# Attention's first two units by pairs of heads, with a new order of the whole program

## The chip, the cores and the metric

The kernel runs on one core of a Trainium2 chip. The metric is the device time of one launch in microseconds (us). A core has five engines that run side by side, each through its own queue in program order: TensorE (PE; its weight loads are PEld) multiplies matrices, VectorE (DVE) and ScalarE (ACT) work on elements, GpSimd (POOL) does the same more slowly, and SyncE (SP) issues the loads and stores (DMAs). PSUM is the memory that TensorE writes its results to; SBUF holds everything else.

## The reference

Local attention with block summaries, then two feed-forward layers, all in fp32.

```python
# q, k, v: (2, 8, 768, 64); block = 32, window = 16
k_sum = k.reshape(B, H, nb, block, D).max(axis=3)
v_sum = v.reshape(B, H, nb, block, D).mean(axis=3)
scores_l = where(abs(i - j) < window, scale * q @ k.T, -1e9)
scores_s = scale * q @ k_sum.T + log(block)
a = softmax(concat(scores_l, scores_s))
x = a @ concat(v, v_sum)                 # reshaped to 1536 tokens x 512
h = x @ w_in                             # 512 x 2048
P = a0 + a1*h + a2*h*h + a3*h**3
Q = 1 + abs(b0)*abs(h) + abs(b1)*h*h
x = (P / (Q + 1e-6)) @ w_out             # 2048 x 512
h = x @ w_in2
out = (h * cos(h)) @ w_out2
```

## The kernel before

**Attention** is cut into units u of 128 queries, all eight heads at once as four pairs (a pair has 2 x 64 = 128 partitions). For the first batch, `k_pair` loads the keys of a pair in two halves of 384 (L454), TensorE turns a half around by six matmuls against the identity, a key group (L463), ScalarE or VectorE copies the result from PSUM into the tile `big` (`cp`, L322 on ScalarE, L324 on GpSimd, L327 on VectorE), and VectorE reduces it to block maxima (L471). `q_tile` brings the queries: for units 0 and 1, one load for heads 0 to 3 and one for heads 4 to 7 hold both units (L559); TensorE turns all four pairs around into one PSUM tile `qtp` of 128x512 (L432), and one copy takes that to `qT`. Later units load `qk` and use L577.

`attn_a` gathers for a unit the 24 block maxima of each head (one copy for all pairs) and the keys in the windows of its two halves of 64 queries (128x768 elements, one copy or two) into `room`, of which there are two sets. Then TensorE makes the scores of all pairs, 16 matmuls into two PSUM tiles `sp` (L626). VectorE masks them pair by pair and takes the minimum (L641; 8 a unit), ScalarE takes the exp (L645), both add and invert the sums (L650, L652, L655), and GpSimd or VectorE multiplies (L658). `attn_b` turns the weights around (`ptp`, L672), `attn_c` loads the values `vw` (L707), multiplies (`avp`, L719) and splits the result into a high and a low part, `xH` and `xL` (L730). `v_mean0` loads v of the first batch (L507), adds neighbours (L514) and makes the block means.

**The layers** multiply in three products of reduced precision (xH with w, xL with w, xH with the low part of w). Weights come as 64 bit floats (`raw`, loaded at L415) and are converted by VectorE in three instructions per 512 columns (L745, L749, L753), cast, and their low part taken on GpSimd or VectorE (L762). `h` is L849 in the first layer and L947 in the second, the second product `acc` is L1091. `co` holds the coefficients (loaded at L380, L381).

**The order.** The functions above do not issue instructions; they write operations with what they read and write into a plan. `ORDER`, a table of numbers (L56), then says for every place in the program which operation comes next and which engine takes it; `add_a` sets the order in which operations are written, on which the table counts. Dependences between operations are kept for named parts of a resource (`Res`), in the plan; the waits in the program are set by what the instructions touch in the tiles. The early PSUM tiles (`ktp`, `qtp`, `sp` and so on, up to unit 1) take the buffers acc0 to acc3 and ps in turn.

## Time and profile before

| | us |
|---|---|
| median of 3 runs (lowest, highest) | 602.42 (601.41 to 603.23) |
| the profiled execution | 601.51 |
| its span | 599.40 |
| outside the span | 2.11 |
| PE busy | 586.1 (98%) |
| DVE busy | 547.9 (91%) |
| ACT busy | 434.2 (72%) |
| POOL busy | 331.8 (55%) |

A row of the stretches gives the busy time of each engine in it, its instructions, the TensorE clock that was granted as a share of full speed, the busy share of the DMA engines and what they moved. A row of the timeline is an instruction or a run of like ones, with its start and its time; in brackets is the idle time of the engine just before it and what ended that. A row of the chain of waits is a piece of the work that ended last. The profile and the times show one core only.

### The profile page before, as it was taken

Reading aid. Unit: us, or ns where it says so; the run is one execution under the profiler, and the core shown is the slowest. Engines: PE = TensorE matmul, PEld = TensorE weight load, DVE = VectorE, ACT = ScalarE, POOL = GpSimd, SP = SyncE. Lnnn points to the kernel's source line nnn. Section 1 sums busy time; section 2 is a strip of 40 time slices with the busy share of each in tenths; the row PEclk is TensorE's granted clock in tenths of the full one; section 3 lists DMA queues with packets and bytes.
Section 4 is the critical chain, followed back from the end, with each engine's and each line's share of the span. In section 5 each row is a group of like instructions: output and inputs, shape, how many; then the busy total and the mean of one; then the engine's idle time right before and its main releaser. Section 6 shows DMA issues by size and latency. Waiting matters only on the chain.

```text
span 599.4 us, 10768 instructions
## 1 busy us (share of the span) xinstructions
PE 586.1 (98%) x3843; PEld 499.7 (83%) x3843; DVE 547.9 (91%) x1082; ACT 434.2 (72%) x940; POOL 331.8 (55%) x317
## 2 busy tenths in 40 slices
PE   8779999999999999999999999999999999999997
PEld 8468878788888888888888888889899989999886
DVE  5899999879999999989999999999889899899784
ACT  3889999677686866887688887675677557754463
POOL 5576876467673666578687733454356617424020
PEclk9899999999999999999999999999999999999999
DMA  8997865200321223321311222021130322200013
GB/s 255 243 240 194 218 185 144 61 1 1 106 71 39 71 68 105 106 71 36 95 46 35 62 80 70 2 71 57 49 107 31 101 78 73 72 1 0 19 71 123
DMA packets 68861, 51.84 MB, mean 86 GB/s; under 512 B 37304, under 2 KB 63160, under 8 KB 68808
## 3 DMA queue, kind: packets, MB, share of 16 engines
q1 hardware_dynamic: 68664, 51.03, 28.8%
q8 instruction: 30, 0.49, 0.3%
q14 instruction: 23, 0.19, 0.1%
q10 hardware_dynamic: 144, 0.13, 0.1%
HBM read 47.71 MB, written 3.15 MB: 85 GB/s over the span
## 4 chain that ended last, share of the span: by engine, by line
PE 89%; DVE 6%; SPq 2%; DMA 1%; ACT 1%; issue 0%; DVEq 0%
PE acc L1091 44%; PE h L849 26%; PE h L947 15%; PE avp L719 1%; PE ptp L672 1%; DMA raw<-in_moe_w_in_dram 1%; PE sp L626 1%; DVE sc L641 1%; DVE f L749 1%; SPq L507 1%; SPq L454 1%; DVE f L753 1%; PE vmp L542 0%; PE qtp L577 0%; DVE f L745 0%
## 5 line engine op out<-in xcount | busy, mean ns | idle before, releaser
L1091 PE MATMUL acc<-gh,w 128*128 128x512 f32 (+1 forms) x416 | 122.8, 378 | 0.0
L1091 PE MATMUL acc<-w,gh 128*128 128x512 f32 x382 | 119.1, 393 | 0.0
L849 PE MATMUL h<-xH,w 128*128 128x512 f32 (+1 forms) x352 | 110.0, 373 | 0.3 <-DVE big L495 0.3
L762 POOL TENSOR_TENSOR gl<-te,gh 128x512 fp32r<-128x512 f32 (+1 forms) x57 | 75.8, 1331 | 47.7 <-ACT gh L322 27.1
L1091 PEld LDWEIGHTS acc<-gh,w 128*128 128x128 f32 x416 | 75.6, 188 | 15.3 <-issue 1.3
L762 POOL TENSOR_TENSOR w<-f,w 128x512 fp32r<-128x512 f32 x47 | 66.3, 1412 | 31.5 <-ACT w L322 25.5
L1008 POOL TENSOR_TENSOR tu<-tu,tf 128x512 f32<-128x512 f32 (+1 forms) x48 | 61.7, 1286 | 32.6 <-ACT tf L1000 31.8
L1091 PE MATMUL acc<-gl,w 128*128 128x512 f32 (+1 forms) x208 | 77.5, 373 | 0.0
L1091 PEld LDWEIGHTS acc<-w,gh 128*128 128x128 f32 x382 | 66.9, 189 | 9.6
L849 PEld LDWEIGHTS h<-xH,w 128*128 128x128 f32 x352 | 64.5, 188 | 12.4 <-DVE big L495 0.5
L1091 PE MATMUL acc<-w,gl 128*128 128x512 f32 x191 | 74.3, 389 | 0.0
L849 PE MATMUL h<-xL,w 128*128 128x512 f32 (+1 forms) x176 | 65.1, 370 | 0.0
L849 PE MATMUL h<-big,w 128*128 128x512 f32 x240 | 58.1, 389 | 0.0
L849 PEld LDWEIGHTS h<-big,w 128*128 128x128 f32 x240 | 45.1, 188 | 9.3
L749 DVE SCALAR_TENSOR_TENSOR f<-raw,f 128x512 int32<-128x512 int32 x64 | 51.1, 800 | 0.4
L753 DVE SCALAR_TENSOR_TENSOR f<-raw,f 128x512 int32<-128x512 int32 x64 | 47.5, 746 | 0.4
L324 POOL TENSOR_SCALAR gh<-te 128x512 fp32r<-128x512 f32 (+1 forms) x26 | 18.9, 728 | 51.0 <-DVE te L1054 20.2
L1091 PEld LDWEIGHTS acc<-gl,w 128*128 128x128 f32 x208 | 39.1, 188 | 6.9
L1049 ACT ACTIVATE h<-h 128x512 f32<-128x512 f32 x48 | 27.9, 582 | 20.7 <-DVE h L1046 20.3
L1091 PEld LDWEIGHTS acc<-w,gl 128*128 128x128 f32 x191 | 35.9, 188 | 7.9
L998 ACT ACTIVATE tu<-h,co 128x512 f32<-128x512 f32 (+1 forms) x52 | 33.6, 651 | 10.9 <-PE h L849 10.8
L1018 ACT ACTIVATE h<-tf 128x512 f32<-128x512 f32 (+1 forms) x52 | 29.7, 571 | 16.2 <-DVE te L1012 15.6
(219 smaller groups left out, 1458.9 us busy)
## 6 DMA issues: line engine op xcount, KB each, us to landing
raw<-in_moe_w_in_dram SPq DMA_DIRECT2D x32, 512.0 KB, 3.7
raw<-in_moe_w_out_dram SPq DMA_DIRECT2D x32, 512.0 KB, 5.1
vw<-in_v_dram SPq DMA_DIRECT2D x24, 192.0 KB, 4.2
qk<-in_q_dram SPq DMA_DIRECT2D x10, 256.0 KB, 5.4
out_dram<-part SPq DMA_DIRECT2D x8, 256.0 KB, 2.0
part<-in_k_dram SPq DMA_DIRECT2D x8, 192.0 KB, 4.0
big<-in_v_dram SPq DMA_DIRECT2D x3, 512.0 KB, 6.6
qk<-in_k_dram SPq DMA_DIRECT2D x6, 256.0 KB, 5.2
```

The lines of the kernel that those rows point to most:

```text
L324: nc.gpsimd.tensor_scalar(out=o, in0=i, scalar1=1.0, scalar2=1.0, op0=ALU.mult, op1=ALU.mult)
L454: lambda e, i=i, rt=rt: nc.sync.dma_start(out=rt(), in_=k[0, 2 * pr:2 * pr + 2, 384 * i:384 * i + 384].rearrange("h (s j) d -> s h (j d)", ...
L749: lambda e: nc.vector.scalar_tensor_tensor(out=ft.t.bitcast(I32), in0=lohi()[1], scalar=-0x40000000, in1=ft.t.bitcast(I32), op0=ALU.bitwis ...
L753: lambda e: nc.vector.scalar_tensor_tensor(out=ft.t.bitcast(I32), in0=lohi()[0], scalar=29, in1=ft.t.bitcast(I32), op0=ALU.logical_shift_r ...
L762: lambda e: E[e].tensor_tensor(out=lo(), in0=x(), in1=hi().bitcast(F32), op=ALU.subtract),
L849: nc.tensor.matmul(out=h.t[:, 0:n], lhsT=lt, rhs=rt[:, kk, cs], start=(k0 == 0 and i == 0), stop=(k0 == 2 and i == 5))
L947: nc.tensor.matmul(out=bank.t[:, c], lhsT=lt, rhs=rt, start=start and i == 0, stop=stop and i == 5, skip_group_check=True)
L998: lambda e: nc.scalar.activation(out=U(), in_=H(), func=ACTF.Square, scale=b1s))
L1008: lambda e: E[e].tensor_tensor(out=U(), in0=U(), in1=Z(), op=ALU.add))
L1018: lambda e: nc.scalar.activation(out=H(), in_=Z(), func=ACTF.Exp, scale=-1.0))
L1049: lambda e: nc.scalar.activation(out=H(), in_=H(), func=ACTF.Abs))
L1091: nc.tensor.matmul(out=dst, lhsT=lt, rhs=rt, start=(un.start and not have and i == 0), stop=(un.stop and i == 2), skip_group_check=have)
```

## The change

`q_tile` for units 0 and 1 makes its transposes and its copy in two halves (pairs 0 and 1, pairs 2 and 3), each half a resource of its own; `attn_a` for these units gathers the block maxima and the windows pair by pair and makes the scores of a pair as soon as its keys and its half of q are there; a mask depends on its pair's scores alone. `add_a` writes `q_tile` of unit 0 behind the first pair of keys. The table `ORDER` is a new one for the whole program, in order and in choice of engine.

```diff
 ORDER = (
-    "c-rk)+mED2bw5?7>bqaMze``fzD@V^^i0pCcRV|L@p^5~nzfg)*S3V$2HUcTu`#SkSm(k;$bcU}0*r`+M8rdau!L}ADT"
...
+    "c-rk*OOIXIRbKmX_IW?=dEMu^kE&bmD&O*>+HH4L+pe}v((P6|3QoE^Qq%4{h(gjhiIfDApcX+4NJk)~NGM8BW)2915s"
...
@@ q_tile
+        dst = qTs[u % NQ]
         if u < 2:
...
+            for i in range(2):
+                def tr(e, i=i):
+                    for x in range(2):
+                        transpose_pairs(tp.t[:, 2 * i + x, :], q_first[i][1]()[:, 2 * x:2 * x + 2], 64 * u, 64)
+
+                P.op([("T", 0.44)], [q_first[i][0]], [tp[i], dst[i]], tr)
+                P.op([("A", act(256, True)), ("V", dve(256))], [tp[i]], [dst[i]],
+                     lambda e, i=i: cp(e, dst.t[:, 2 * i:2 * i + 2], tp.t[:, 2 * i:2 * i + 2]))
+            P.now += 0.88
+            return
...
@@ attn_a
+        every = range(NP)
+
+        def gather(prs):
+            sl = slice(prs[0], prs[-1] + 1)
+            np_ = len(prs)
+            kks = {kr["k", i, y] for w in ws for i in range(w // 128, (w + WK - 1) // 128 + 1) for y in prs}
...
+            if t < NKW:
+                sums = [kr[x] for x in kr.subs if x[0] == "s" and x[1] in prs]
+                P.op([("P", Shared(0.6 if np_ == NP else 0.22)), ("A", act(48 * np_))], sums, [kw["s", y] for y in prs],
+                     lambda e: cp(e, kw.t[:, sl, :, WK:KW],
+                                  ks()[:, sl].unsqueeze(2).to_broadcast([128, np_, 2, NB])))
+            n = 192 * np_
+            P.op([("P", Shared(0.85 if np_ == NP else 0.18 + n * 0.00087)), ("A", act(n)), ("V", dvef(n))],
+                 sorted(kks, key=id), [kw["w", y] for y in prs], windows)
+            P.op([("T", SPT * np_ / NP)], [qt[i] for i in sorted({y // 2 for y in prs})] + [kw[x, y] for x in "sw" for y in prs],
+                 [sp[y] for sp in sps for y in prs], mm)
+
+        if u < 2:
+            for y in every:
+                gather([y])
+        else:
+            gather(list(every))
...
-                P.op([("V", 0.19)], [sp, m], [sc[pr], mn[hh, pr]],
+                P.op([("V", 0.19)], [sp[pr], m], [sc[pr], mn[hh, pr]],
...
@@ add_a
         if u == 0:
-            for i in range(NP):
+            fill.append((k_pair, 0, 30.0))
+            fill.append((q_tile, 0, 30.0))
+            for i in range(1, NP):
                 fill.append((k_pair, i, 30.0))
...
-        fill.append((q_tile, u, 30.0 if u < 2 else 8.0))
+        if u:
+            fill.append((q_tile, u, 30.0 if u < 2 else 8.0))
```

Three places show how the new table moves instructions; the lines of the changed code are by one to 16 higher. The first is TensorE at the start of the program, before: key groups (`ktp`) up to the last two, then the transposes of q; in brackets is what an instruction waits for.

```order
L463 MATMUL ktp<-ident,part 64x128 [waits DMAHW6_49,DVE_49]
L463 MATMUL ktp<-ident,part 64x128 x5
L463 MATMUL ktp<-ident,part 64x128 [waits DMAHW7_49,DVE_49]
L463 MATMUL ktp<-ident,part 64x128 x5
L432 MATMUL qtp<-ident,part 64x64 [waits DMAHW1_49,DVE_49]
L432 MATMUL qtp<-ident,part 64x64 x7
L432 MATMUL qtp<-ident,part 64x64 [waits DMAHW0_49]
L432 MATMUL qtp<-ident,part 64x64 x7
```

And the changed program, TensorE from the first key group, and, behind "...", from the first scores to the last key group:

```order
L464 MATMUL ktp<-ident,part 64x128 [waits DMAHW2_49]
L464 MATMUL ktp<-ident,part 64x128 x5
L433 MATMUL qtp<-ident,part 64x64 [waits DMAHW3_49,DVE_49]
L433 MATMUL qtp<-ident,part 64x64 x7
...
L627 MATMUL sp_273<-room,qT_203 64x120 [waits Activation_49]
...
L433 MATMUL qtp<-ident,part 64x64 [waits DVE_49]
L433 MATMUL qtp<-ident,part 64x64 x7
L433 MATMUL qtp<-ident,part 64x64 [waits Activation_49]
L433 MATMUL qtp<-ident,part 64x64 x7
L464 MATMUL ktp<-ident,part 64x128 [waits DMAHW1_49,DVE_49,PE_49]
L464 MATMUL ktp<-ident,part 64x128 x5
```

All four halves of q and the scores of unit 0's first pair now stand ahead of the last key group; the second half of unit 0 waits for VectorE, that of unit 1 for ScalarE. Second, ScalarE at the start, before: copies of key groups, the block maxima into `room`, one copy of q, and then the exps (L645).

```order
L330 ACT_TABLE_LOAD
L322 COPY big<-ktp 128x384 x5
L322 COPY room<-big 128x8x24
L322 COPY qT_307<-qtp 128x512
L645 ACTIVATE sc,su<-sc,mn 128x120 x11
L322 COPY qT_282<-qtp 128x512
```

And changed, from the third key copy to the copy of q for unit 2:

```order
L323 COPY big<-ktp 128x384
L323 COPY room<-big 128x2x24
L323 COPY big<-ktp 128x384
L323 COPY qT_289<-qtp 128x256 x2
L323 COPY room<-big 128x2x24 x3
L323 COPY room<-big 128x96 x2
L323 COPY big<-ktp 128x384
L323 COPY room<-big 128x2x24 x2
L661 ACTIVATE sc,su<-sc,mn 128x120 x11
L323 COPY qT_203<-qtp 128x512
```

Five small copies stand between the second half of unit 1's q and the last copy of keys, two more behind it, and the exps come after. Third, SyncE's loads, before: keys, q, v, the q of unit 2 (`qk`), the coefficients, the first w_in (`raw`).

```order
L454 DMA part<-in_k_dram 128x2x192 x8
L559 DMA part<-in_q_dram 128x4x128 x2
L507 DMA big<-in_v_dram 128x8x128 x3
L415 DMA qk<-in_q_dram 128x8x64
L380 DMA co<-in_moe_a_dram 128x4
L415 DMA raw<-in_moe_w_in_dram 128x4x128
L707 DMA vw_356<-in_v_dram 96x8x64
```

And changed:

```order
L455 DMA part<-in_k_dram 128x2x192
L560 DMA part<-in_q_dram 128x4x128
L455 DMA part<-in_k_dram 128x2x192
L560 DMA part<-in_q_dram 128x4x128
L455 DMA part<-in_k_dram 128x2x192 x6
L508 DMA big<-in_v_dram 128x8x128 x3
L416 DMA raw<-in_moe_w_in_dram 128x4x128
L381 DMA co<-in_moe_a_dram 128x4
L416 DMA qk<-in_q_dram 128x8x64
L723 DMA vw_388<-in_v_dram 96x8x64
```

The loads of q stand behind the first and the second piece of keys, and w_in and the q of unit 2 have changed places. Of the window copies, those of units 0 and 1 are now 96 or 2x96 columns wide and spread over the three engines; the 128x768 copies of units 2, 3 and 4 are on GpSimd, VectorE and ScalarE, where they were on GpSimd, GpSimd and ScalarE.

## Rows read from the trace of the kernel before

**Rows 1.** Page, and stretches: window, us, busy PE PEld DVE ACT POOL, PEclk, DMA

```profile
PE 586.1 (98%) x3843; PEld 499.7 (83%) x3843; DVE 547.9 (91%) x1082; ACT 434.2 (72%) x940; POOL 331.8 (55%) x317
60.00:590.00 530.00, 529.88 (x3123) 453.12 (x3121) 494.77 (x888) 387.11 (x776) 293.53 (x252) 1.00 0.23 69
```

**Rows 2.** Stretches from 20 to 60 us

```profile
20.00:25.00 5.00, 3.42 (x67) 3.05 (x68) 4.43 (x18) 4.17 (x15) 1.58 (x2) 0.80 0.77 210
...
30.00:60.00 30.00, 25.62 (x331) 22.09 (x332) 29.77 (x110) 28.06 (x102) 22.19 (x27) 1.00 0.83 217
```

**Rows 3.** Chain of waits, 5 to 32 us: start, us, what

```profile
10.85 1.45 SPq L415
...
13.87 6.61 DMA raw<-in_moe_w_in_dram
```

**Rows 4.** Timeline of PE: start, us, line and operation, [idle before, releaser]

```profile
5.14 6.00 PE L463 MATMUL ktp<-ident,part 128*64 128x128 f32 x96
11.07 1.91 PE L432 MATMUL qtp<-ident,part 64*64 64x64 f32 x64
13.11 1.87 PE L626 MATMUL sp<-room,qT 64*64 64x120 f32 x64
...
17.78 0.66 PE L577 MATMUL qtp<-ident,qk 128*128 128x128 f32 x4
...
23.22 2.17 PE L719 MATMUL avp<-pt,vw 120*64 120x64 f32 x32 [0.88 <-DMA vw<-in_v_dram]
...
27.61 1.15 PE L719 MATMUL avp<-pt,vw 120*64 120x64 f32 x30 [0.17 <-ACT pt L322]
...
31.11 0.38 PE L849 MATMUL h<-xH,w 128*128 128x256 f32 x1
```

**Rows 5.** Timeline of DVE, the same columns

```profile
6.44 0.56 DVE L327 COPY big<-ktp 128x384 f32<-128x384 f32 x1 [6.44 <-PE ktp L463]
6.92 0.55 DVE L471 TENSOR_REDUCE big<-ktp 128x12 f32<-128x384 f32 x1
...
13.94 0.69 DVE L514 TENSOR_TENSOR big<-big 128x512 f32<-128x512 f32 x1 [0.38 <-DMA big<-in_v_dram]
14.55 0.27 DVE L641 CUSTOM_DVE_ANT_0 sc<-sp,room 128x120 f32<-128x120 f32 x1
...
17.27 0.31 DVE L652 TENSOR_SCALAR su<-su 128x4 f32<-128x4 f32 x1 [0.21 <-ACT sc L645]
...
20.50 0.43 DVE L745 TENSOR_SCALAR f<-raw 128x512 int32<-128x512 int32 x1 [0.99 <-DMA raw<-in_moe_w_in_dram]
...
23.91 0.40 DVE L327 CAST w<-f 128x512 fp32r<-128x512 f32 x1
```

**Rows 6.** Timeline of ACT, the same columns

```profile
10.53 0.48 ACT L322 COPY big<-ktp 128x384 f32<-128x384 f32 x1 [0.18 <-PE ktp L463]
11.18 0.48 ACT L322 COPY big<-ktp 128x384 f32<-128x384 f32 x1 [0.18 <-PE ktp L463]
12.28 0.35 ACT L322 COPY room<-big 128x192 f32<-128x192 f32 x1 [0.62 <-DVE big L471]
...
14.86 0.40 ACT L645 ACTIVATE sc<-sc,mn 128x120 f32<-128x120 f32 x1 [1.25 <-DVE mn L641]
...
19.04 0.56 ACT L322 COPY qT<-qtp 128x512 f32<-128x512 f32 x1
...
21.29 0.39 ACT L645 ACTIVATE sc<-sc,mn 128x120 f32<-128x120 f32 x1 [0.55 <-DVE mn L641]
...
23.27 0.21 ACT L650 ACTIVATE su<-su 128x4 f32<-128x4 f32 x1
23.37 0.82 ACT L322 COPY room<-big 128x768 f32<-128x768 f32 x1
```

**Rows 7.** Page, DMA issues: instruction, count, KB each, median us to landing

```profile
raw<-in_moe_w_in_dram SPq DMA_DIRECT2D x32, 512.0 KB, 3.7
...
qk<-in_q_dram SPq DMA_DIRECT2D x10, 256.0 KB, 5.4
```

More of the change, by code (lines that the diff above doesn't have):

```diff
@@ L618, in attn_a @@
-        n = 768
-        P.op([("P", Shared(0.85)), ("A", act(n)), ("V", dvef(n))], sorted(kks, key=id), [kw["w"]], windows)
-        def mm(e):
-            for pr in range(NP):
-                for half in range(2):
-                    for hh in range(2):
-                        p0, c0 = 64 * hh, 64 * half
-                        nc.tensor.matmul(out=sps[hh].t[c0:c0 + 64, pr, :],
-                                         lhsT=qt.t[p0:p0 + 64, pr, c0:c0 + 64],
-                                         rhs=kw.t[p0:p0 + 64, pr, half, :], start=True, stop=True)
@@ L630, in attn_a, with windows, mm @@
-        P.op([("T", SPT)], [qt, kw["s"], kw["w"]], sps, mm)
+        every = range(NP)
[3 more added lines that the diff above has]
+            kks = {kr["k", i, y] for w in ws for i in range(w // 128, (w + WK - 1) // 128 + 1) for y in prs}
+            def windows(e):
+                if ws[1] - ws[0] == 64:
+                    x = kk()[:, sl, ws[0]:ws[0] + 128].rearrange("p n (a s) -> p n a s", a=2)
+                    x = bass.AP(x.tensor, x.offset, [x.ap[0], x.ap[1], x.ap[2], [1, WK]])
+                    cp(e, kw.t[:, sl, :, 0:WK], x)
+                else:
+                    for half in range(2):
+                        cp(e, kw.t[:, sl, half, 0:WK], kk()[:, sl, ws[half]:ws[half] + WK])
+            def mm(e):
+                for pr in prs:
+                    for half in range(2):
+                        for hh in range(2):
+                            p0, c0 = 64 * hh, 64 * half
+                            nc.tensor.matmul(out=sps[hh].t[c0:c0 + 64, pr, :],
+                                             lhsT=qt.t[p0:p0 + 64, pr, c0:c0 + 64],
+                                             rhs=kw.t[p0:p0 + 64, pr, half, :], start=True, stop=True)
+            if t < NKW:
[8 more added lines that the diff above has]
+                 [sp[y] for sp in sps for y in prs], mm)
```

135 lines of the change are left out of this document (58 added, 77 removed).

## Prediction

> **What bounds the kernel now.** I read the totals and the long stretches first [rows 1]. TensorE is busy 586.1 of 599.4 us; from 60 to 590 us it is busy 529.88 of 530 us, so nothing can be gained there except by taking work from it, and this change leaves its matmul work after 60 us alone. What can move is the first 60 us, where the change also has its instructions; the 9.4 us behind 590 us it leaves as they are, so what comes in between moves as a block. Second, the first 60 us in stretches [rows 2]: from 20 to 25 us TensorE works 3.42 of 5 us, at a granted clock of 0.80, so part of it at 1.2 GHz and not 2.4. From 30 to 60 us VectorE is busy 29.77 of 30 us. So VectorE, not TensorE, decides how soon the full stretch begins: a us by which VectorE is later at 30 us is a us at the end, and one it saves is saved there. Third, the chain of waits between 11 and 31 us [rows 3]: the issues on SyncE from 10.85 on, the first w_in load (issued 13.87, 6.61 us), and from its landing VectorE. The first part of attention is off that chain by little: VectorE's idle time ahead of 20.50 is 0.99 us, and ScalarE waits 0.55 us at 21.29 [rows 5, 6]. I therefore cost the change in two chains: when the masks of unit 0 can start, and when w_in is there.
>
> **Term 1, when attention starts.** Before, TensorE makes eight key groups from 5.14 to 11.07, then four groups of q (1.91, so 0.48 a half tile), then 32 score matmuls (1.87, so 0.23 for a pair) [rows 4]. Late key groups come 0.66 us apart, as ScalarE's copies at 10.53 and 11.18 show [rows 6]. The first mask is at 14.55 on VectorE, the first exp at 14.86 on ScalarE [rows 5, 6]; VectorE is tied there by the v add, which waits for its load until 13.94 and lasts to 14.55.
> In the changed order all four q halves and the scores of one pair stand ahead of the last key group. That moves 1.91 + 0.23 = 2.14 us of TensorE in front of it, 11.07 to 13.21, and brings two waits that before has not. The second half of q's transposes writes the same PSUM tile whose first half is being copied, and the order shows TensorE waiting there on VectorE for unit 0 and on ScalarE for unit 1. For unit 0: the first key group is copied at 6.44 and reduced from 6.92 to 7.47 [rows 5]; the q half follows, at 256 of the 384 columns that take 0.56, so 0.40, and ends near 7.8. TensorE has reached the second half at 6.22 + 0.48 + 0.66 = 7.36 (the first key group ends 0.22 ahead of its copy at 6.44), so it stands about 0.5 us. For unit 1, ScalarE must copy the seventh key group (0.48) and then the q half (0.38, by the same scaling) while TensorE needs 0.48 for that half: about 0.7 us. One TensorE group is also saved from earlier stalls (the first groups came 0.74 us apart on the average, 0.66 later), about 0.2. The last key group then ends at 13.21 + 0.5 + 0.7 - 0.2 = 14.2 instead of 11.07.
> Behind that wait stand the last key group's copy and its reduction. ScalarE first has the second q half (to about 14.1) and five small copies. Before shows no copy of 48 or 96 columns there; the nearest rows are 0.21 for 4 columns, which costs the engine 0.10 to the next start, and 0.35 for 192 [rows 6], so five cost 0.5 to 1.2 us; three of them have 48 columns, so I take 0.7. The copy then runs 14.7 to 15.2, VectorE's reduction (0.55) to 15.77, and the first mask starts at about 15.7: **+1.15 us**, with 1.0 and 1.7 as ends. The small window copies on VectorE (four of 96 columns, each under the 0.40 that 512 columns take [rows 5]) fall in times when it waits for key groups, and so do those on GpSimd; were that cover gone they would cost up to 4 x 0.40 = 1.6.
>
> The Trainium skill's page "PSUM — Partial Sum Buffer", section "PSUM bank collisions raise a hardware error", speaks against splitting the tile: two engines may not be in one bank and partition quadrant at once, even at different columns, so PSUM is to be guarded by bank. By it both waits bind and term 1 stands; a kernel guarded by halves would save the 1.2 us of them. No run here shows a collision.
>
> **Term 2, the weights come sooner.** SyncE now issues w_in directly behind the v loads, where the load of q for unit 2 stood (10.85 instead of 13.87 [rows 3]). With the same 6.61 us it is there at 17.5, before VectorE can use it. That takes away VectorE's 0.99 us at 20.50; the 0.21 us at 17.27 [rows 5] goes as well, because the masks there are now behind ScalarE by less. **-1.20 us**; ScalarE's 0.55 us at 21.29 is the same loss seen from the other engine and isn't counted again. The least is 0.2, if VectorE then waits for exps instead: 16 exps at 0.38 a piece (11 from 14.86 to 19.04 [rows 6]) from 16.0 end at 22.1.
>
> **Term 3, work that changes engines.** One window copy of 128x768 moves from GpSimd to VectorE. A 512-column copy from SBUF takes VectorE 0.40 (at 23.91), and of one instruction 0.08 lies beside the next (6.44 to 6.92 for one of 0.56 [rows 5]); so 768 take 1.5 x 0.32: **+0.48 us**, from 0 (hidden in a remaining wait) to 0.6. From about 25 us on, both orders have nearly the same rows, so they carry the shift. Later, ten more casts of gh go to VectorE (17 by the changed order, 7 before); TensorE is full there and VectorE has room (494.77 of 530 us [rows 1]), so they cost nothing; without that cover they would cost 10 x 0.40, 4 us.
>
> **Term 4, the price of term 2.** The load of q for unit 2 is now behind w_in and the coefficients, issued near 13.87. Loads of this kind take 5.4 us at the median and the one of w_in at that time 6.61 [rows 3, 7], so it lands between 19.3 and 20.5. TensorE had transposed it at 17.78, ScalarE copied it at 19.04, after 11 exps [rows 4, 6]. With the exps 1.15 later, ScalarE comes to that copy at 20.2, and the transposes (0.66) want the data by 19.3. So the stall is 0 to 1.2 us; behind it on ScalarE stand the last exps of unit 1, on TensorE the transposes of unit 0's weights, and VectorE waits for both. I take 0, as the median lands on the edge, and keep 1.2.
>
> **Sum.** +1.15 - 1.20 + 0.48 + 0 = +0.43 on the profiled execution of 601.51 us (span 599.40 and 2.11 around it): 601.9. That execution is 0.91 below the median of 602.42, so the forecast is 602.42 + 0.43, **602.8 us**. In its own range, 601.4 to 604.2, are 0.55 more at the start, 1.2 of term 4, and 1.0 less if VectorE also loses waits of the next units. A measurement of this kernel tells about 0.3%, 1.8 us, from no change.
>
> **Rivals.** A, faster: the pairs do what they are for. VectorE's row at 13.94 speaks for it: the v add ties VectorE until 14.55 in any case, so if the waits in the halves are shorter than I have them and the last key group comes in time, the start doesn't move (0). Then -1.20 + 0.48, and TensorE, which idles less between 18 and 24 us, keeps the full clock: the attention product at 23.22 took 2.17 us where the next, at 27.61, took 1.15 for two fewer of 32 instruction pairs [rows 4], so 1.0 less. -1.7, and up to -2.2 if the window copy is hidden: about 600.5. Against it: TensorE must do 2.14 us more ahead of the last key group, whatever the waits. Chance 0.20.
> B, slower: the late q of unit 2. It decides if that load lands after 19.3. Then 1.2 us on ScalarE and TensorE's queue add to term 1, TensorE idles there and the following product and transposes run again at 1.2 GHz, 1.0 more: +0.43 + 1.2 + 1.0 = +2.6, 605.0. For it: the load's place, and a granted clock of 0.80 already [rows 2]. Against it: w_in needs not be as slow as 6.61 (its median is 3.7 [rows 7]), and all behind it then lands sooner. Chance 0.25.
> C, the change does not do what it says: scores by pairs bring no earlier mask, since VectorE stands at the v add and the reduction of the last group either way, and the rest of the order is the same. It is 0 to +0.4 and lies within the forecast.
>
> **How the numbers follow.** Forecast with C 0.55, A 0.20, B 0.25. The range reaches from A's middle to B's: 600.4 to 605.0; only the outer halves of A and B are left out. Faster by over 0.3% (under 600.6) is A, 0.20; slower (over 604.2) is B, 0.25; the same is 0.55.
>
> **What would show it.** In the profile after: the first mask at 15.7 and the first exp at 16.0 (A: 14.6 and 14.9); TensorE's q groups split by two waits of 0.5 and 0.7 on copies; no idle time of VectorE before the first conversion of w_in; ScalarE's copy of q for unit 2 at about 20.2 without a wait (B: a wait of up to 1.2 on TensorE's transposes, and these on the load); the first matmul of h, 31.11 before [rows 4], at 31.5 (A: 29.5, B: 33 or later); from 60 to 590 us TensorE full. It would be wrong if key or q pieces, in their new order, land after TensorE wants them, if VectorE has idle time between 30 and 60 us that takes up a shift, or if the casts on VectorE open gaps on TensorE.

## The result, and the profile after

The changed kernel takes 604.42 us (median of 20 runs, 602.74 to 608.78), the kernel before, run beside it, 602.17 (20 runs, 600.79 to 603.84). The ratio is 1.0051, with an interval of 1.0037 to 1.0064: slower by 2.3 us between the medians and by 3.1 by the ratio. The forecast was 602.8, "the same". Of the 20 runs after, 8 took over 605 us; the experiments come back to these. The profiled execution after took 603.46 us with a span of 601.70, 2.30 more than the span before.

The page's totals of the changed kernel:

```profile
PE 586.5 (97%) x3843; PEld 498.9 (83%) x3843; DVE 548.6 (91%) x1081; ACT 431.4 (72%) x945; POOL 334.3 (56%) x330
```

The stretches of the changed kernel that answer to [rows 1, 2] (window, us, busy PE PEld DVE ACT POOL, clock, DMA share, GB/s):

```profile
20.00:25.00 5.00, 3.71 (x48) 2.31 (x46) 4.87 (x15) 4.44 (x19) 1.00 (x2) 1.00 0.59 135
...
0.00:60.00 60.00, 49.49 (x689) 40.49 (x690) 51.05 (x196) 46.65 (x169) 36.71 (x67) 1.00 0.83 228
60.00:100.00 40.00, 38.97 (x490) 32.47 (x490) 37.26 (x145) 37.28 (x137) 31.23 (x34) 1.00 0.75 196
100.00:590.00 490.00, 490.00 (x2630) 419.60 (x2629) 457.60 (x738) 344.94 (x638) 265.10 (x230) 1.00 0.19 59
```

The same stretches of the kernel before:

```profile
0.00:60.00 60.00, 50.57 (x697) 42.15 (x698) 50.99 (x193) 46.09 (x163) 38.28 (x66) 0.97 0.87 233
60.00:100.00 40.00, 39.88 (x493) 33.27 (x491) 38.45 (x152) 37.88 (x134) 31.00 (x33) 1.00 0.76 203
```

From 100 to 590 us TensorE is full in both kernels. So the difference is TensorE's idle time ahead of 100 us: 60 - 49.49 = 10.51 us against 9.43 in the first 60 us, **+1.08**, and 1.03 against 0.12 in the next 40, **+0.91**. The rest of the 2.30 is 0.38 us more of TensorE's own busy time (586.49 against 586.11 us), less 0.07 of idle time behind 590 us. The second loss has two addresses, 0.59 us at 93.66 and 0.32 at 79.71. For the larger one, the timeline of VectorE, changed kernel (start, us, line and operation, [idle before, releaser]):

```profile
92.31 0.43 DVE L761 TENSOR_SCALAR f<-raw 128x512 int32<-128x512 int32 x1 [1.15 <-DMA raw<-in_moe_w_out_dram]
...
92.94 0.66 DVE L746 TENSOR_TENSOR xL<-avp,xH 128x512 fp32r<-128x512 f32 x1
```

And TensorE, the smaller wait and then the larger:

```profile
79.71 1.09 PE L582 MATMUL qtp<-ident,qk 128*128 128x128 f32 x8 [0.32 <-ACT pt L323]
...
93.66 0.50 PE L865 MATMUL h<-xH,w 128*128 128x512 f32 x1 [0.59 <-DVE xL L746]
```

VectorE stands 1.15 us for a load of `w_out`; behind that conversion in its queue is the split of the attention product into `xL`, for which the next matmul of `h` waits. (The wait at 79.71, for a copy on ScalarE, comes back as 0.3 us in every profile below that has the changed order here: e2, e3, e5, e7, e9, e13 to e16 and e18. No run takes it apart.) The load comes late because of its place, as e3 will show. SyncE's issues there, after:

```profile
86.12 0.46 SPq L416 DMA_DIRECT2D raw<-in_moe_w_in_dram  x1
86.69 0.93 SPq L416 DMA_DIRECT2D raw<-in_moe_w_out_dram  x2
```

And before:

```profile
84.77 1.32 SPq L415 DMA_DIRECT2D raw<-in_moe_w_out_dram  x2
86.18 0.38 SPq L415 DMA_DIRECT2D raw<-in_moe_w_in_dram  x1
```

The new table puts the 512 KB of `w_in` ahead of the two pieces of `w_out` that VectorE wants first.

The start of the changed kernel. TensorE, answering to [rows 4]:

```profile
6.54 0.68 PE L433 MATMUL qtp<-ident,part 64*64 64x64 f32 x16
7.15 0.88 PE L464 MATMUL ktp<-ident,part 128*64 128x128 f32 x12
8.06 0.68 PE L433 MATMUL qtp<-ident,part 64*64 64x64 f32 x16
...
13.47 0.68 PE L433 MATMUL qtp<-ident,part 64*64 64x64 f32 x16 [0.47 <-ACT qT L323]
14.08 0.88 PE L464 MATMUL ktp<-ident,part 128*64 128x128 f32 x12
...
20.58 0.66 PE L582 MATMUL qtp<-ident,qk 128*128 128x128 f32 x4
...
25.50 1.15 PE L735 MATMUL avp<-pt,vw 120*64 120x64 f32 x30 [0.51 <-ACT pt L323]
...
32.25 0.39 PE L865 MATMUL h<-xH,w 128*128 128x256 f32 x1
```

ScalarE, answering to [rows 6]:

```profile
14.46 0.84 ACT L323 COPY room<-big 128x48 f32<-128x48 f32 x5
15.21 0.48 ACT L323 COPY big<-ktp 128x384 f32<-128x384 f32 x1
...
16.58 0.39 ACT L661 ACTIVATE sc<-sc,mn 128x120 f32<-128x120 f32 x1
```

VectorE, answering to [rows 5]:

```profile
15.71 0.56 DVE L472 TENSOR_REDUCE big<-ktp 128x12 f32<-128x384 f32 x1 [0.64 <-ACT big L323]
16.19 0.27 DVE L657 CUSTOM_DVE_ANT_0 sc<-sp,room 128x120 f32<-128x120 f32 x1
...
18.65 0.82 DVE L328 COPY room<-big 128x768 f32<-128x768 f32 x1
...
22.11 1.18 DVE L761 TENSOR_SCALAR f<-raw 128x512 int32<-128x512 int32 x1
```

And GpSimd beside that last row:

```profile
22.02 0.99 POOL L674 TENSOR_TENSOR sc<-sc,su 128x480 f32<-128x480 f32 x1 [2.96 <-DVE su L671]
```

The first mask is at 16.19 (14.55 before, +1.64), the first exp at 16.58 (+1.72), the first matmul of `h` at 32.25 (+1.14). Between the first mask and the first `h`, 0.50 us is won back; VectorE's own account of that stretch shows how, after:

```profile
16.19:32.25 16.06, 15.90 (x75) 1.00 0.77 199
```

And before:

```profile
14.55:31.11 16.56, 14.96 (x77) 0.90 0.93 248
```

Here the columns are window, us, busy DVE, clock, DMA share, GB/s. VectorE's idle time fell from 1.60 to 0.16 us (-1.44), and its work grew by 0.94. So +1.64 - 1.44 + 0.94 = +1.14.

These are two executions, and the start varies between executions. With the old start the first `h` comes at 30.33 to 31.11 (before and, below, e2, e10 and e12), with the new one at 31.79 to 32.43 (after, e1, e3 and e5); the two ranges do not meet.

### The profile page after: what moved, and what is told of

The parts are those of the page before. It is cut to its first block, busy times and chain, and to the rows that moved or that the text cites. A ratio compares the mean times of both kernels' runs of the same rounds, so it can differ in the third digit from the quotient of the medians.

```text
span 601.7 us, 10801 instructions
## 1 busy us (share of the span) xinstructions
PE 586.5 (97%) x3843; PEld 498.9 (83%) x3843; DVE 548.6 (91%) x1081; ACT 431.4 (72%) x945; POOL 334.3 (56%) x330
## 4 chain that ended last, share of the span: by engine, by line
PE 89%; DVE 8%; DMA 1%; ACT 1%; issue 0%; POOL 0%; POOLq 0%; DVEq 0%
PE acc L1107 43%; PE h L865 26%; PE h L963 15%; DVE sc L657 1%; PE ktp L464 1%; DMA raw<-in_moe_w_out_dram 1%; PE avp L735 1%; PE sp L627 1%; PE ptp L688 1%; DVE f L765 1%; DVE f L761 1%; DVE f L769 1%; PE warm L357 1%; DVE xL L746 1%; DVE big L496 0%; PE vmp L543 0%
## 5 line engine op out<-in xcount | busy, mean ns | idle before, releaser
L778 POOL TENSOR_TENSOR gl<-te,gh 128x512 fp32r<-128x512 f32 (+1 forms) x54 | 69.9, 1294 | 63.3 <-ACT gh L323 25.3
L778 POOL TENSOR_TENSOR w<-f,w 128x512 fp32r<-128x512 f32 x44 | 61.7, 1404 | 31.0 <-DVE w L328 16.6
L1024 POOL TENSOR_TENSOR tu<-tu,tf 128x512 f32<-128x512 f32 (+1 forms) x45 | 58.0, 1289 | 33.2 <-ACT tf L1016 33.1
L1031 ACT ACTIVATE tf<-tu 128x512 f32<-128x512 f32 (+1 forms) x52 | 31.4, 603 | 14.9 <-POOL tu L1024 11.2
```

Of the source, the lines that this page charges most:

```text
L778: lambda e: E[e].tensor_tensor(out=lo(), in0=x(), in1=hi().bitcast(F32), op=ALU.subtract),
L1024: lambda e: E[e].tensor_tensor(out=U(), in0=U(), in1=Z(), op=ALU.add))
L1031: lambda e: nc.scalar.activation(out=Z(), in_=U(), func=ACTF.Ln, bias=QC))
```

## The experiments

Theory at the outset: two separate losses, the start and the order of loads near 86 us. The rival: the start alone, and what stands behind is its echo. Later ones are named where they arise. The edits are to the table `ORDER` (in e4, e11 and e17 also to `add_a`, which writes `q_tile` where it stood before), so they are shown as rows of an engine's queue; "after" is the changed kernel. Beside each stood 13 to 35 runs of before, with medians of 601.70 to 602.12.

**The two halves of the order.** e1 takes the changed order up to about 58 us and the old one behind; e2 the old start and the changed order behind.

> The changed kernel with its own order up to the second key tile of the second batch (about 58 us) and, from there on, the order and the engines of the kernel before. Theory S (two separate losses: the start by pairs, 1.1 us at the first matmul of h, and the new order behind 60 us, 0.9 us in two waits of TensorE at 79 and 93 us): slower than before by 1.1 to 1.4 us, no TensorE wait between 70 and 100 us. Rival E (one loss: the late start eats the slack, and the later waits are its echo): slower by 2.0 to 2.5 us, with TensorE waits between 70 and 100 us again.

> The kernel before, with its own order up to the same place (about 58 us), and from there on the order and engines of the changed kernel. Theory S: slower than before by 0.9 to 1.2 us, with TensorE waits near 78 and 92 us. Rival E: no change, within 0.3 us, and no TensorE wait between 70 and 100 us.

e1: 602.93, ratio 1.0016 (1.0004 to 1.0028). e2: 602.19, 1.0011 (0.9995 to 1.0026). So the start costs some 0.16%; e2 can't be told from nothing. The profiles fit neither theory well. That of e1 is of its longest run (605.43, the others have 602.16 to 603.68): TensorE stands 1.4 us at 61.95, where the two orders are joined, and 1.2 at 98.30 for a load of `vw`, where theory S had no wait between 70 and 100 us. In e2 only the wait of 0.3 near 78 us is there; VectorE waits 0.6 us for `w_out`, and TensorE doesn't stand for it.

**The changed kernel again (e5)**, unedited, to see how it varies.

> The changed kernel itself, once more, beside the three others. In 8 of 20 executions it took 605.6 us or more, in the others 602.7 to 604.7; with the one load moved (the run before) 12 of 12 stayed at 604.0 or below. Theory L (the load order at 86 us is what makes part of the executions slow, by how late that w_out load lands): again some executions over 605.5, median 603.4 to 605. Rival (a chance of that chip or hour): all within 602.5 to 604.5 and a median within 0.5 us of the one with the load moved.

603.38 (602.67 to 607.65), ratio 1.0020 (1.0004 to 1.0036), below the first measurement of the same kernel; the two intervals don't meet. The reason is in how the runs are spread: of the 32 runs of both series, 10 took 605.66 to 608.78 us; the others have a median of 603.47. The profile of e5 is of such a long run (607.22). TensorE's longest wait in it behind 60 us (engine, tile and line, what it waited for: us, times, longest):

```profile
PE h L865 <- DVE xL L746: 2.7, 1, 2.7
```

VectorE's, of the same run:

```profile
DVE f L761 <- DMA raw<-in_moe_w_out_dram: 3.2, 1, 3.2
```

And its stretch:

```profile
60.00:100.00 40.00, 36.88 (x447) 30.77 (x446) 34.88 (x142) 34.27 (x130) 29.52 (x33) 0.96 0.71 189
```

It is the wait of 93 us again, 3.2 instead of 1.15 us long; TensorE is idle for 3.12 us of the stretch instead of 1.03, its start is the same (idle 10.47 us, 10.51 after). So in this long run the late load is simply later. Of its 3.76 us over the profiled execution of after, 2.09 are this idle time and 1.73 are longer busy time of TensorE, with a granted clock of 0.96 in the stretch. The other nine long runs have no profile.

**The loads put back (e3).** After, with the two loads in the old sequence:

```diff
 DMA vw<-big 24x512
+DMA raw<-in_moe_w_out_dram 128x512 x2
 DMA raw<-in_moe_w_in_dram 128x4x128
-DMA raw<-in_moe_w_out_dram 128x512 x2
 DMA vw<-in_v_dram 96x8x64
```

> The changed kernel, where one load changes its place on SyncE: the w_in load that is issued at 86.1 us comes behind the two w_out loads at 86.7 instead of ahead of them, as in the kernel before. Theory L (VectorE's 1.15 us of idle time at 92.3 and TensorE's wait of 0.59 at 93.1 come from that place): the wait at 93 us is gone, 0.5 to 0.7 us faster than the changed kernel, +1.7 us against before. Rival: the waits come from the work that is late anyway (the xH cast and the weights behind the exps), and the time stays at +2.3 us.

602.65 (602.05 to 604.02), ratio 1.0014 (1.0001 to 1.0027). TensorE's only wait behind 60 us:

```profile
PE qtp L580 <- ACT pt L321: 0.3, 1, 0.3
```

And the stretch:

```profile
60.00:100.00 40.00, 39.56 (x493) 33.11 (x491) 38.47 (x148) 37.84 (x136) 31.14 (x34) 1.00 0.76 201
```

The wait for `xL` is gone, and TensorE's idle time is 0.44 us instead of 1.03. In the medians that is 0.7 us against e5, whose interval meets e3's, and 1.8 against the first series, whose interval doesn't. Clearer than the medians are the long runs: none over 605 us here, nor in two further kernels below with this sequence and the same start (e9, e14), 0 of 36 against 10 of 32. A run over 605 us doesn't name this load by itself: kernels with the old sequence and another start have such runs too (before, e1, e6, e7, e13, e15, e16, e18).

**The same swap in the kernel before (e10)**, `w_in` ahead of the two `w_out`, nothing else.

> The kernel before with one load moved the other way: near 85 us the w_in load comes ahead of the two w_out loads, as in the changed kernel. Theory L (a w_out load that stands behind another 512 KB is late for VectorE, whatever the start): VectorE waits 1 to 3 us for it near 90 us, +0.5 to +1.5 us at the median and some executions 3 us or more above the rest. Rival (it hurts only together with the late start, which has used up the slack): within 0.3 us of before.

602.92, ratio 1.0022 (1.0002 to 1.0042), and 4 of 12 runs over 604.5, against 2 of 31 of before beside it. VectorE's wait is there although the start is the old one:

```profile
DVE f L744 <- DMA raw<-in_moe_w_out_dram: 1.0, 1, 1.0
```

TensorE stands 0.35 us for the conversions behind it, and its idle time from 60 to 100 us is 0.56 (0.12 in before). So the load order costs something by itself, and the rival that it hurts only with the late start falls, though narrowly (the interval begins at 1.0002, and in e2 TensorE had no such wait). That the late start makes the same wait dearer isn't excluded.

**Term 2 alone (e6).** Before, with the first `w_in` and the coefficients issued ahead of the q of unit 2:

```diff
+DMA raw<-in_moe_w_in_dram 128x4x128
+DMA co<-in_moe_a_dram 128x4
 DMA qk<-in_q_dram 128x8x64
-DMA co<-in_moe_a_dram 128x4
-DMA raw<-in_moe_w_in_dram 128x4x128
```

> The kernel before, with one thing of the change: on SyncE the first w_in load stands directly behind the v loads, then the first coefficients, then the load of q for unit 2. Theory of the prediction (terms 2 and 4): VectorE's 0.99 us of idle time ahead of its first conversion goes, -1.0 us, less up to 1.2 us for the later q of unit 2: between -1.0 and +0.2 us. Rival P (the exps on ScalarE pace VectorE there, so the idle time only moves to a later place): 0, within 0.3 us, with VectorE waiting for exps or TensorE instead.

602.26, ratio 1.0004 (0.9984 to 1.0024): nothing. TensorE's timeline:

```profile
23.44 1.15 PE L718 MATMUL avp<-pt,vw 120*64 120x64 f32 x32 [0.77 <-DVE su L654]
...
29.33 1.15 PE L625 MATMUL sp<-room,qT 64*64 64x120 f32 x32 [1.09 <-ACT qT L321]
30.79 0.36 PE L848 MATMUL h<-xH,w 128*128 128x256 f32 x1 [0.31 <-DVE mn L640]
```

VectorE no longer waits for `w_in`, but the first `h` comes only 0.32 us sooner (31.11 before), less than it varies with the old start unedited (30.33 to 31.11): other waits, for sums and for the q of a later unit, take the place of that one.

**The code without the order (e4).** The split code of the change, in the old order and with the old engines.

> The changed code (keys gathered, q copied and scores made by pairs in the first two units), but in the order and on the engines of the kernel before: all key groups first, then q, each piece where the whole stood. It isolates the splitting from the new order. Theory (the split alone costs fixed time per piece and hides nothing): the eight window copies of 96 columns on GpSimd take longer than the two of 384 before, the first mask is 0.4 to 1.0 us later, the first matmul of h too, so +0.3 to +1.0 us. Rival (the pairs pipeline by themselves, the loss lies in where q and the scores were put): the first mask 0.3 to 0.6 us earlier, and the time 0 to 0.5 us shorter.

601.71 (599.46 to 604.45), ratio 0.9994 (0.9977 to 1.0011). Its first mask is at 14.65, nearly as before (14.55). Splitting q, windows and scores shows no cost; what costs is the order.

**Term 3 undone (e9).** e3, with the 128x768 window copy of VectorE back on GpSimd.

> The changed kernel with the load moved as before, and the window copy of unit 3 (128x768) on GpSimd as in the kernel before, in place of VectorE. Theory W (term 3: the copy costs VectorE 0.74 us on the path): first matmul of h 0.5 to 0.8 us earlier, time 0.3 to 0.8 us below the kernel with the load moved alone. Rival (the masks wait for scores and exps at that place, so the copy fills a hole): no change within 0.3 us.

602.29 (601.90 to 603.17), ratio 0.9995 (0.9981 to 1.0010), 0.36 below e3 and not to be told from before, and the first `h` no earlier (32.35; 31.79 in e3, whose first key copy is 1.03 us sooner). VectorE is spared 0.74 us of copy, but a scaling of 4 columns behind the masks now lasts 0.83 us instead of 0.16, until 20.05, and GpSimd's two window copies run from 18.39 to 20.02.

**GpSimd's neighbour taken away (e18).** In after, and in e9 at 22.20, the first conversion of `w_in` takes 1.18 us instead of 0.43 while GpSimd multiplies unit 0's weights. e18 is e9 with that multiply on VectorE:

```diff
 VectorE TENSOR_TENSOR sc<-sc,su 128x480
+VectorE TENSOR_TENSOR sc<-sc,su 128x480
 VectorE TENSOR_SCALAR f<-raw 128x512
 ...
-GpSimd TENSOR_TENSOR sc<-sc,su 128x480 x3
+GpSimd TENSOR_TENSOR sc<-sc,su 128x480 x2
```

> e9 (loads near 86 us put back, unit 3's window copy on GpSimd) with one more edit: the multiply of unit 0's weights that GpSimd makes at 22.11 us, 0.99 long, is made by VectorE (0.65), ahead of the first conversion of w_in, which took 1.18 us there instead of 0.43. Theory L, that VectorE's instruction is held until GpSimd's ends: the conversion takes 0.4 to 0.45 again, VectorE gains 0.75 and pays 0.58 for the multiply, the first h comes at 32.2 (32.35 in e9) and the time is e9's, 602.1 to 602.4. The rival, that the conversion is long for a reason of its own (its data, its place behind the masks): it still takes 1.1 to 1.2, VectorE is 0.6 later, the first h near 32.9 and the time near 602.9.

The conversion, on VectorE:

```profile
22.78 0.42 DVE L759 TENSOR_SCALAR f<-raw 128x512 int32<-128x512 int32 x1
```

So theory L holds: it was held by GpSimd. But the time is 603.78 (10 runs), ratio 1.0036 (1.0020 to 1.0053), slower than e9, and the first `h` of the profiled execution comes at 35.27, which neither theory expected. The multiply pushes one mask from 22.00 to 22.57; ScalarE waits 0.60 us for it, and its copy of `vw`, behind the exps, comes later. TensorE:

```profile
25.18 0.33 PE L733 MATMUL avp<-pt,vw 120*64 120x64 f32 x2 [1.49 <-ACT vw L321]
...
29.78 1.97 PE L733 MATMUL avp<-pt,vw 120*64 120x64 f32 x30 [0.27 <-ACT pt L321]
```

It stands 1.49 us there (0.95 in e9 and in after), and the same product that takes 1.15 in those takes 1.97. The stretch:

```profile
30.00:35.00 5.00, 4.33 (x66) 3.77 (x65) 3.24 (x12) 3.89 (x19) 2.26 (x2) 0.50 0.86 235
```

Behind half a us more of idle time the granted clock was 0.70 from 25 to 30 us and 0.50 from 30 to 35, the lower level of 1.2 GHz; in e9 and after it was 1.00 in both. This profiled execution is one of three of the ten near 605.5 us (605.83; the others have 603.25 to 603.81), so these stretches show the loss of the clock for it alone. The mean granted clock over the span is on record for every run: 0.991 to 0.992 in these three, 0.996 to 0.997 in the other seven, 0.999 to 1.000 in all twelve of e9. So how much of the median's 1.5 us over e9 is the later mask, and how much the clock, stays open.

**Which piece of the start it is.** Theory Q said the q of unit 1, ahead of the last key group; theory K, that all q halves are ahead of keys; another, the wait in one PSUM tile; another, the five small copies on ScalarE. One kernel for each. e7 is e3 with the last key group, its copy and its reduction ahead of unit 1's q:

```diff
-MATMUL ktp<-ident,part 64x128 x30
+MATMUL ktp<-ident,part 64x128 x36
 MATMUL sp<-room,qT 64x120
 ...
 MATMUL qtp<-ident,part 64x64 x16
-MATMUL ktp<-ident,part 64x128 x6
```

> The changed kernel with the load moved as before (w_out ahead of w_in near 86 us), and the last key group, its copy on ScalarE and its reduction on VectorE put ahead of the transposes of unit 1's q, as the kernel before has them. Theory Q (what makes the start late is what stands ahead of the last key group: two q halves, 0.96 us, and TensorE's wait of 0.47 for ScalarE): first mask 1.0 to 1.4 us earlier than in the changed kernel relative to its first key group, first matmul of h 0.8 to 1.3 us earlier, time 0.4 to 1.2 us below the kernel with the load moved alone. Rival (the small copies on ScalarE and GpSimd hold the start): the first mask stays within 0.3 us and the time too.

604.56, ratio 1.0037 (1.0023 to 1.0051), slower than e3. The key group then stands itself, and q comes later. The profile names no releaser; in the program this group waits for a reduction on VectorE that reads the PSUM buffer it will write:

```profile
13.46 0.88 PE L462 MATMUL ktp<-ident,part 128*64 128x128 f32 x12 [1.22 <-issue]
```

e13 is e9 with all eight key groups and their loads ahead of all halves of q:

```diff
-MATMUL ktp<-ident,part 64x128 x6
-MATMUL qtp<-ident,part 64x64 x8
-MATMUL ktp<-ident,part 64x128 x6
-MATMUL qtp<-ident,part 64x64 x8
-MATMUL ktp<-ident,part 64x128 x30
+MATMUL ktp<-ident,part 64x128 x48
+MATMUL qtp<-ident,part 64x64 x32
```

> The changed kernel with w_out ahead of w_in near 86 us and the third unit's second window copy on GpSimd (602.29 us in its run), where in the first 15 us all eight key groups, their copies and reductions stand ahead of all four q halves, and the loads of keys ahead of those of q, as in the kernel before; the engines of all pieces and the rest stay those of the change. Theory K (q among the key groups makes the keys late, and VectorE idles for them): VectorE's idle time for ScalarE's key copies between 8 and 16 us falls from about 2 to below 1 us, first matmul of h at 30.5 to 31.3 instead of 32.3, time 0.5 to 1.2 us less. Rival (the many small copies on ScalarE and VectorE make the start late): first matmul of h within 0.4 us of 32.3, the same time.

606.26 (8 runs), ratio 1.0058 (1.0036 to 1.0080). VectorE's first mask:

```profile
18.52 0.28 DVE L655 CUSTOM_DVE_ANT_0 sc<-sp,room 128x120 f32<-128x120 f32 x1 [3.05 <-PE sp L625]
```

The keys are through early, but now the halves of q alternate with their copies (TensorE waits 0.93 and 0.47 us for them), with nothing in between to fill the waits. Both theories fall: the mixed order is not the fault in itself, it hides these waits. They are the smaller part of the loss: of the 3.80 us over e9's profiled execution (602.90), 1.43 are idle time of the first 60 us and 2.30 longer busy time of TensorE, at a granted clock of 0.94 there.

e14 is e9 with both halves of unit 1's q turned around in a row, and copied after. The rows are the same; the wait inside the tile (here with what each row waits for) is gone:

```diff
 MATMUL qtp<-ident,part 64x64 [waits DVE_49]
-MATMUL qtp<-ident,part 64x64 x7
-MATMUL qtp<-ident,part 64x64 [waits Activation_49]
-MATMUL qtp<-ident,part 64x64 x7
+MATMUL qtp<-ident,part 64x64 x15
```

> The kernel of the run with the third unit's second window copy on GpSimd (the changed kernel, w_out ahead of w_in near 86 us; 602.29 us in its run), with one thing more: TensorE makes both halves of q for a unit in a row, and the copies of the halves follow. Theory B (the wait of TensorE for the copy of the first half, 0.47 us at 13.5 us, holds the start): no wait of TensorE in q, last key group 0.4 to 0.6 us earlier, first matmul of h 0.3 to 0.6 us earlier, time 0.2 to 0.6 us less. Rival (ScalarE, which copies both halves and then makes five small copies, holds the start): the first mask within 0.2 us, the same time.

602.42, ratio 1.0004 (0.9986 to 1.0022), as e9. TensorE, and VectorE's first mask:

```profile
13.50 0.88 PE L462 MATMUL ktp<-ident,part 128*64 128x128 f32 x12
```

```profile
15.88 0.27 DVE L655 CUSTOM_DVE_ANT_0 sc<-sp,room 128x120 f32<-128x120 f32 x1
```

The last key group starts 0.6 us sooner than after's, the first mask 0.3, the first `h` (31.87) 0.5 sooner than e9's; the time doesn't move. e15 is e9 with ScalarE's small copies on GpSimd, nine by the trace, of which the five that stand in a row are shown (e16 has e14's edit as well):

```diff
-ScalarE COPY room<-big 128x2x24 x3
-ScalarE COPY room<-big 128x96 x2
+GpSimd TENSOR_SCALAR room<-big 128x2x24 x3
+GpSimd TENSOR_SCALAR room<-big 128x96 x2
```

> The same base, with the eight small copies of units 0 and 1 that ScalarE makes (five of block maxima, three of windows) on GpSimd instead, which makes most of them in the kernel before. Theory A (ScalarE's small copies stand ahead of its copy of the last key group, 0.74 us, and hold the first mask): the last key group's copy 0.5 to 0.8 us earlier, first matmul of h 0.4 to 0.9 us earlier, time 0.3 to 0.8 us less. Rival (GpSimd is slower per piece, and the scores wait for it instead): the first mask the same or up to 1 us later, time 0 to +1.0 us.

> Both of these: q's halves in a row on TensorE, and ScalarE's eight small copies on GpSimd. If each alone moves the start, first matmul of h 0.8 to 1.4 us earlier than in the base, at about 31, and the time 0.5 to 1.2 us less, near 601.5. If one chain only takes the place of the other, no more than the better of the two.

607.36 and 607.19 (6 runs each), ratios 1.0074 (1.0048 to 1.0100) and 1.0078 (1.0054 to 1.0102). TensorE's scores wait for GpSimd (e15):

```profile
17.25 1.30 PE L625 MATMUL sp<-room,qT 64*64 64x120 f32 x32 [1.65 <-POOL room L323]
```

Because there the last small copies stand behind the add of v, which itself waits for its load:

```profile
15.74 1.26 POOL L513 TENSOR_TENSOR big<-big 128x512 f32<-128x512 f32 x1 [0.24 <-DMA big<-in_v_dram]
16.96 1.08 POOL L323 TENSOR_SCALAR room<-big 128x48 f32<-128x48 f32 x5
```

**A better one (e11, e17).** e4 with the two `w_out` loads issued still earlier, ahead of four small copies on SyncE; e17 is the same kernel, measured again. e12 gives that edit to before.

```diff
 DMA qk<-in_q_dram 128x8x64 x2
+DMA raw<-in_moe_w_out_dram 128x512 x2
 DMA vw<-big 24x512
 ...
-DMA raw<-in_moe_w_out_dram 128x512 x2
 DMA raw<-in_moe_w_in_dram 128x4x128
```

> The pairs in the order of the kernel before (601.71 us in its run), with the two w_out loads of the 85th us issued ahead of the four small copies of v's block means on SyncE, so up to 3.5 us earlier. Theory L: the spread of the executions (599.5 to 604.5) shrinks from above, as loads no longer land late: median 600.5 to 601.3, no execution over 603. Rival (the spread has another source, such as the first loads or the clock): median 601.4 to 602.1 and the same spread.

> The kernel before with the same two w_out loads ahead of the four small copies on SyncE. Theory L: 0.3 to 1.0 us below before, fewer executions over 603. Rival: no change, within 0.3 us.

> Once more the pairs in the order of the kernel before, with the two w_out loads of the 85th us ahead of the four small copies (601.46 us against 601.7 for before in its run, ratio 0.9987 with an interval from 0.9972 to 1.0002). If it is faster than both kernels, again 0.2 to 1.0 us below before and no execution over 603; if that was chance, within 0.2 us of before.

e11: 601.46, ratio 0.9987 (0.9972 to 1.0002). e17: 600.69 (599.89 to 602.03), 0.9980 (0.9964 to 0.9996), against 601.78 of before beside it. e12: 602.59, 1.0009 (0.9996 to 1.0022). So the split code in the old order with earlier loads is the fastest of all, by 0.1 to 0.2%; e11 by itself can't be told from before, e17 can. The early loads alone don't make before faster, and whether they add to e4 (0.9994) isn't shown, as the intervals overlap. e17's stretch:

```profile
60.00:100.00 40.00, 40.00 (x494) 33.50 (x492) 38.38 (x151) 37.47 (x133) 31.15 (x33) 1.00 0.76 202
```

TensorE's account in eight profiled executions, in us (the idle times from the stretches, as above):

| kernel | time | idle, 0 to 60 | idle, 60 to 100 | busy in all |
|---|---|---|---|---|
| before | 601.51 | 9.43 | 0.12 | 586.11 |
| after | 603.46 | 10.51 | 1.03 | 586.49 |
| e5, after, a long run | 607.22 | 10.47 | 3.12 | 588.22 |
| e3, loads put back | 602.19 | 9.91 | 0.44 | 586.41 |
| e13, keys first | 606.70 | 12.00 | 0.49 | 588.78 |
| e18, multiply on VectorE | 605.83 | 9.84 | 0.61 | 589.95 |
| e4, pairs, old order | 600.04 | 9.22 | 0.00 | 585.41 |
| e17, and early loads | 600.18 | 9.73 | 0.00 | 585.03 |

Idle time and busy time together leave 5.4 us of each but before (5.9): every profiled time is made of those two.

## Why the prediction was wrong

**The first 60 us: the direction was right, the size was not.** The start was to move by +1.15 - 1.20 + 0.48 = +0.43; it moved by +1.14.

*Term 1*, +1.15, measured +1.64 at the first mask, at the far end of its bounds (1.0 to 1.7). TensorE gets to the last key group 8.94 us after the first (5.14 to 14.08); seven groups at the old pace are 7/8 of 5.93, or 5.19, so the moved work took 3.75 us, where the sum had 2.14 + 0.5 + 0.7 - 0.2 = 3.14. The waits were overestimated: only unit 1's is there, 0.47. The work was underestimated: a half of q among key groups takes 0.61 to the next start (6.54 to 7.15, 8.06 to 8.68), not 0.48, and the key group between two of them 0.91, not 0.74. The price of a group, taken from a row where 64 like matmuls follow one another, doesn't hold where short groups alternate; two halves of q in a row, in e14, take 1.03. The granted clock is 1.00 in all these rows. The five small copies were right (0.75 for 0.7). Nor was there one piece to blame at the end: without the wait in the tile (e14) the mask comes 0.3 us sooner and the time stays; each other piece that was moved (e7, e13, e15) made a new wait at the next link, from TensorE over ScalarE's copy and VectorE's reduction to the scores.

The rule of the Trainium skill that was weighed there ("PSUM — Partial Sum Buffer", "PSUM bank collisions raise a hardware error") asks that such a tile be guarded by bank; here that guard is a wait of 0.47 us, and e14 shows that its removal by another sequence is worth nothing.

*Terms 2 and 3.* VectorE's waits did go, even more of them than forecast: its idle time between the first mask and the first `h` fell by 1.44 us (1.20 forecast). But VectorE was to be the bound there, and on such an engine idle time is a gain only if no work takes its place. Its work grew by 0.94: the window copy took 0.74 to the next start (18.65 to 19.39), not 0.48, since I scaled it from a cast of 512 columns; and the first conversion of `w_in` took 1.18 us, not 0.43, beside a multiply of GpSimd that ran from 22.02 to 23.01. The rest of its work was 0.55 less. That last cost was in no term; e18, which takes that neighbour away, has 0.42. **The failed step is the one that took an instruction's duration as fixed, while the order decides what GpSimd does beside it.** The Trainium skill states the mechanism ("SBUF — State Buffer", "SBUF: two separate sides"): VectorE and GpSimd share a pair of ports as an exclusive lock, for VectorE's instructions in a two-port mode or with two inputs in SBUF, and the one that comes second is blocked until the other's instruction is over. In which mode this conversion runs, no run here shows. The trace agrees roughly: VectorE's instruction of 0.43 us ends 0.28 us after GpSimd's of 0.99, so by the records 0.15 of it ran beside that one; GpSimd's times are the rough ones of a profile. What the cost is worth at the end isn't shown, as e18 was slower for other reasons.

Nor was the -1.20 to be had by itself: in e6, on the old start, it brought 0.32 us at the first `h`, within the spread, and nothing at the end.

*The sum itself.* It adds term 1 to the rest, as if a us at the first mask were a us at the first `h`. One profile speaks against that. In e10, which has the old start, a load of v came late in the profiled execution and held the first mask until 16.19, as late as after's, and the first `h` still comes at 31.01. Its first mask, VectorE's account from there to the first `h`, and that `h`:

```profile
16.19 0.27 DVE L640 CUSTOM_DVE_ANT_0 sc<-sp,room 128x120 f32<-128x120 f32 x1
...
16.19:31.01 14.82, 14.21 (x74) 1.00 0.94 248
...
31.01 0.38 PE L848 MATMUL h<-xH,w 128*128 128x256 f32 x1
```

So behind the same mask the old order needs 14.82 us and the new one 16.06 (15.99 to 16.07 in e1, e3, e5, e9 and e14), with 14.21 and 15.90 us of work on VectorE. The old order had room for a late mask; the new one has none, because VectorE's work fills it. That work, more than the later mask, is what the new start lost. No run was made for this, and it is one execution.

**Behind 60 us: the step that failed.** I wrote that both orders have "nearly the same rows" from about 25 us on, and that TensorE is full from 60 to 590, so that nothing there can be gained. So the sum has no term for that part: it was put at nothing. TensorE was full there in before, but the rows were not looked at closely enough, and what is full can still be opened. One pair of loads, exchanged on SyncE near 86 us, makes VectorE wait for 1.15 us and TensorE for 0.59, up to 3.2 and 2.7 in a long run; another 0.32 is the wait for ScalarE at 79.71. Together that is +0.91 of the 2.30 us in the profiled execution, and the loads are most of what lifts the median to 604.42: e3 (loads put back) takes 1.8 us off it, or 0.7 off the second series, and e10 (the same swap in before) adds 1.2 to before. The rows of the change that I went by show SyncE's queue only at the start. The ten more casts on VectorE show no cost: from 100 to 590 us TensorE is full.

**The rivals.** B named the right side for a wrong reason: the q of unit 2 was in time, its transposes at 20.58 wait for no load, so term 4 at 0 was right. A's gain did come in part: the granted clock from 20 to 25 us is 1.00 (0.80 before), and the attention product takes 1.15 us. But VectorE, with next to no idle time there, was later than before, and TensorE stood 0.95 and 0.51 us around that product for copies on ScalarE, so the faster product brought nothing forward. What the clock is worth is seen where it is lost: the profiled execution of e18 took 605.83 us, that of e9 602.90, with 3.47 us more of TensorE's busy time and 0.55 less of its idle time ahead of 100 us. C was partly right: pairs bring no earlier mask, in the old order either (14.65 in e4).

**Of what I said would show it**: the missing idle time of VectorE ahead of the first conversion is there, of the two waits between the halves of q only one; mask, exp and copy of q came 0.5, 0.6 and 1.1 us later than said (16.19, 16.58, 21.28), the first `h` 0.75; from 60 to 590 TensorE was to be full and is busy 528.97 of 530 us, where 529.88 was before. The forecast's own range was also added up wrongly: 0.55, 1.2 and 1.0 were put on 602.42, the time before, which gives its 601.4 to 604.2; on the forecast they give 601.8 to 604.6.

What stays open: the shares of the start's 1.1 us among its links, and why that load landed 2 us later in e5's profile. The medians of e3 and e9 put the start at only some 0.5 us over before, the ratio of e9 (0.9995) at nothing, where the idle times of the profiles have 0.5 to 1.1; VectorE's first copy of keys, which follows the first load, begins at 5.70 (e3) to 6.74 us (e5, e10).

## What to carry to other kernels

When an order is searched anew, compare every load queue over the whole program, also where the bound engine is full: one exchange of two loads cost, by the medians, no less (0.7 to 1.8 us) than the part that was rewritten (some 0.5). On an engine that sets the pace, count work and idle time together, and look at what its neighbour on the shared ports does at that moment. Before you take a mixed order apart, find out which waits it hides: all six kernels that moved one piece of this start (e7, e13 to e16, e18) were slower than the order they were to mend, or no faster.

## What the runs showed of the hardware

A VectorE instruction can last some three to five times as long beside GpSimd: 1.18 us for one of 0.43 (0.42 without the neighbour), 0.83 for one of 0.16 (e9). It does not beside every instruction of GpSimd: in before the same conversion takes 0.42 at 25.03, with GpSimd busy from 24.07 to 26.59. The same load landed about 2 us later in one execution of a kernel (e5) than in another (after); 10 of 32 runs with this order of loads were some 3.5 us longer than the rest, and none of 36 with the other order and the same start. And idle time of TensorE can be paid twice: behind a wait that was 0.54 us longer than e9's in e18's profiled execution the granted clock fell to 0.50 for the next stretch, and TensorE's busy time was 3.5 us over after's for the same matmuls; in e5, which has a wait of 2.7 us, 1.7.
